# Loading the row-sum reciprocals with one broadcast DMA per head instead of one per two heads

## Chip, cores and metric

The kernel runs on 1 core of one Trainium2 chip. The metric is device microseconds of one execution, from inputs in the chip's memory to the output in it. Three runs of the kernel before are given, and one profiled execution of it.

## What is computed

Three parts follow each other: a masked attention over 4 batches, 8 heads, 576 rows and 64 columns a head, a gated unit, and a bilinear unit. All is in float32. Cut to what matters:

```python
scores = scale * q @ k.T
thresh = max(scores) - tau
attn = exp(where(scores >= thresh, scores, -1e9) - max(scores))
attn = attn / (sum(attn) + 1e-09)
x = attn @ v                                  # [2304 tokens, 512]
x = (silu(x @ w_gate) * (x @ w_val)) @ w_out  # gated unit
out = ((x @ w1) * (x @ w2)) @ w3 @ w_out2     # bilinear unit
```

## The kernel before

Float32 products are made from three matmuls each (`mm3`, line 814): every operand is split into a rounded high part and a low part, and high by high, high by low and low by high are added up in PSUM.

**Attention** goes through 16 pairs of heads (4 batches by 4 pairs). VectorE takes row maxima (L467) and masks (L486, which also writes the row sums), ScalarE takes the exponentials, TensorE transposes and multiplies by v (L565, L570). The product is not yet divided by its row sum. It leaves PSUM as two halves, which `it_pv` stores to the DRAM tensor `x_dram` (index e = 0, 1, L581). After the last pair of a batch `it_norm` takes the reciprocals of the row sums, turns them and stores them to `r_dram`, one row of 576 values for each batch and head (L596, L599).

**Between attention and gated unit** stands `x_prep(j, kk)`. The 2304 tokens are cut into five blocks j of 512, 512, 256, 512 and 512 tokens, and the 512 features into four groups kk of 128, which are two heads of 64 features each. `x_load` takes two tiles ("slots") from a list of free ones and loads into the first both halves from `x_dram` (L770), and into the second the reciprocals from `r_dram` (L774): the row of one head goes to each of the partitions 0 to 63, the row of the next head to each of the partitions 64 to 127, all in one DMA. A block that crosses a batch border does this in two segments (448 and 64 tokens, or 128 and 128). Then GpSimd adds the two halves (L805), VectorE multiplies by the reciprocals (L808), the two loaded slots are given back, ScalarE rounds the high part (L796) and VectorE subtracts to get the low part (L797). There are 20 such steps and 32 segments.

**The gated unit** goes through pairs g of 128-column groups f, and for each g through the five blocks. In the first pair (g = 0) `glu_step(0, j, f)` multiplies block j and prepares two of the four groups kk of block j + 1 (L923). So the blocks of x are made while the first pair is multiplied, and the later pairs find them there. `glu_h` makes the gated product (L898, L899) and splits it, with GpSimd on L106; `glu_out` multiplies it by `w_out` into `s_bank`.

**Weights** are loaded as raw words (`conv_load`, L127) into three buffers, and converted a step at a time (`conv_step`: VectorE L138 to L156, ScalarE L147, L148 and L195, GpSimd L149 and L198).

**Order.** Every data DMA of the kernel is issued from the SP queue, one after the other. The order of each engine's instructions is set by a scheduler when the program is built, so one more DMA can move others. The first step of block 0 and the first weights are prepared while attention runs (`early`), the first two steps of the gated unit in its tail.

Of the kernel before, what the change touches and what calls it, by code (L numbers as in the profile page):

```python
# [35 lines left out]
def kernel(  # L36
# [21 lines left out]
    nc = tc.nc  # L58
# [22 lines left out]
    r_dram = dram.tile([B, H, S], F32, name="r_dram")  # L81
# [93 lines left out]
    def take(dt=F32R):  # L175
        pool, tag = free.popleft()
        t = pool.tile([P, 2, 512], dt, tag=tag, name=tag, bufs=1)
        owner[id(t)] = (pool, tag, t)
        return t
# [574 lines left out]
    def segs(c0, n):  # L754
        done = 0
        while done < n:
            b, c = divmod(c0 + done, S)
            m = min(n - done, S - c)
            yield done, b, c, m
            done += m  # L760
# [4 lines left out]
    def x_load(j, kk):  # L765
        c0, n = blocks[j]
        x_raw[j, kk] = [take(F32) for _ in range(2)]
        tt, rg = x_raw[j, kk]
        for o, b, c, m in segs(c0, n):
            nc.sync.dma_start(  # L770
                out=tt[:, :, o:o + m],
                in_=x_dram[:, kk * P:(kk + 1) * P, b, c:c + m].rearrange("e p c -> p e c"),
            )
            nc.sync.dma_start(  # L774
                out=rg[:, 0, o:o + m],
                in_=r_dram[b, 2 * kk:2 * kk + 2, c:c + m].unsqueeze(1).to_broadcast([2, 64, m]),
            )
        return tt, rg

    def x_views(j):  # L780
# [20 lines left out]
    def x_prep(j, kk):  # L801
        c0, n = blocks[j]
        tt, rg = x_load(j, kk)
        xr = tmp()
        nc.gpsimd.tensor_tensor(  # L805
            out=xr[:, 0:n], in0=tt[:, 0, 0:n], in1=tt[:, 1, 0:n], op=ALU.add
        )
        nc.vector.tensor_tensor(out=xr[:, 0:n], in0=xr[:, 0:n], in1=rg[:, 0, 0:n], op=ALU.mult)  # L808
        give(*x_raw.pop((j, kk)))
        x_split(j, kk, xr[:, 0:n])  # L810
# [170 lines left out]
    for i in range(NF2):  # L981
        conv_until((i, 1), w3v)
        bank = t_bank()
        for c in range(NF2):
# [8 lines left out]
            out=un[:, 1, :], in0=bank, in1=f32(un[:, 0, :]), op=ALU.subtract  # L993
# [109 lines left out]
```

## Time and profile before

| | |
|---|---|
| median of 3 runs | 1231.96 us (1230.54 to 1233.79) |
| profiled execution, its time | 1231.65 us |
| profiled execution, its span | 1229.9 us |
| mean granted TensorE clock | 0.971 |
| busy in the span: PE, DVE, POOL, ACT | 1114.0, 788.0, 604.7, 563.0 us |

The span is from the first to the last instruction; some 1.7 us of the execution's time lie around it. PE is TensorE, DVE is VectorE, ACT is ScalarE, POOL is GpSimd, and SPq is the SP queue, which issues the DMAs. A busy share is an average over stages with different limits, so the rows below are taken by stage: up to about 347 us attention alone, from 347 to 402 us its tail with the first steps of the gated unit, then to 478 us the first pair of the gated unit, and from there on matmuls almost without a gap. The granted clock is given as a share of 2.4 GHz, so 0.50 is 1.2 GHz. The DMA share is the mean busy share of the core's 16 DMA engines; packets that overlap count each, so it can stand above 1.

### The profile page before, as it was taken

Reading aid. Unit: us, or ns where it says so; the run is one execution under the profiler, and the core shown is the slowest. Engines: PE = TensorE matmul, PEld = TensorE weight load, DVE = VectorE, ACT = ScalarE, POOL = GpSimd, SP = SyncE. Lnnn points to the kernel's source line nnn. Section 1 sums busy time; section 2 is a strip of 40 time slices with the busy share of each in tenths; the row PEclk is TensorE's granted clock in tenths of the full one; section 3 lists DMA queues with packets and bytes.
Section 4 is the critical chain, followed back from the end, with each engine's and each line's share of the span. In section 5 each row is a group of like instructions: output and inputs, shape, how many; then the busy total and the mean of one; then the engine's idle time right before and its main releaser. Section 6 shows DMA issues by size and latency. Waiting matters only on the chain.

```text
span 1229.9 us, 16704 instructions
## 1 busy us (share of the span) xinstructions
PE 1114.0 (91%) x5972; PEld 952.0 (77%) x5972; DVE 788.0 (64%) x1303; ACT 563.0 (46%) x1010; POOL 604.7 (49%) x602
## 2 busy tenths in 40 slices
PE   7888878888777845999999999999999999999998
PEld 5877777778666644888888888888877888888886
DVE  7999999999988635756546373548795021432223
ACT  6777667777755522634234242335474241231211
POOL 7999989999975423533323142324342131231110
PEclk9999999999978967999999999999999999999999
DMA  9856656555444544321102021113431010000014
GB/s 203 202 134 148 146 132 149 129 131 133 106 133 134 140 118 131 103 69 52 53 18 69 18 69 52 52 35 103 127 107 58 1 35 1 18 18 1 1 52 103
DMA packets 104370, 107.07 MB, mean 87 GB/s; under 512 B 47328, under 2 KB 78688, under 8 KB 104288
## 3 DMA queue, kind: packets, MB, share of 16 engines
q1 hardware_dynamic: 104288, 106.01, 33.2%
q8 instruction: 47, 0.77, 0.3%
q14 instruction: 35, 0.29, 0.1%
HBM read 68.16 MB, written 14.23 MB: 67 GB/s over the span
## 4 chain that ended last, share of the span: by engine, by line
PE 55%; DVE 15%; POOL 13%; DMA 8%; issue 3%; SPq 3%; ACT 1%; DVEq 0%; POOLq 0%; ACTq 0%
PE t_bank L814 36%; PE s_bank L814 18%; DVE P L486 5%; POOL AT L102 4%; DMA slot<-r_dram 3%; DVE P L467 3%; POOL AT L99 3%; DMA raw<-in_moe_w_gate_dram 2%; POOL AT L517 2%; DMA raw<-in_moe_w_dram 2%; POOL stat L459 2%; SPq L770 1%; DVE tmp L156 1%; DVE slot L797 1%; DVE tmp L144 1%
## 5 line engine op out<-in xcount | busy, mean ns | idle before, releaser
L814 PE MATMUL t_bank<-slot,slot 128*128 128x512 f32 (+1 forms) x2592 | 566.3, 374 | 25.2 <-ACT slot L796 14.1
L814 PEld LDWEIGHTS t_bank<-slot,slot 128*128 128x128 f32 x2592 | 461.4, 191 | 113.2 <-ACT slot L796 14.7
L486 DVE SCALAR_TENSOR_TENSOR P<-P,stat,E 128x576 f32<-128x576 f32 x144 | 184.2, 1303 | 1.6 <-POOL stat L459 1.3
L814 PE MATMUL s_bank<-h,slot 128*128 128x512 f32 (+1 forms) x720 | 163.6, 376 | 16.6 <-POOL h L106 15.6
L149 POOL TENSOR_TENSOR raw<-raw 128x512 int32<-128x512 int32 x76 | 86.9, 1144 | 159.7 <-ACT raw L148 149.2
L814 PEld LDWEIGHTS s_bank<-h,slot 128*128 128x128 f32 x720 | 128.7, 194 | 40.9 <-POOL h L106 16.5
L1043 POOL TENSOR_TENSOR h<-tmp,h 128x512 fp32r<-128x512 f32 (+1 forms) x38 | 45.8, 1204 | 200.5 <-ACT h L1041 200.5
L106 POOL TENSOR_TENSOR h<-tmp,h 128x512 fp32r<-128x512 f32 (+1 forms) x60 | 73.5, 1225 | 136.5 <-ACT h L105 136.4
L1039 DVE TENSOR_TENSOR tmp<-tmp,t_bank 128x512 f32<-128x512 f32 (+1 forms) x40 | 25.3, 633 | 178.3 <-PE t_bank L814 178.3
L476 ACT ACTIVATE E<-P,stat 128x576 f32<-128x576 f32 x144 | 112.6, 789 | 54.6 <-DVE P L467 27.9
L428 PE MATMUL s_bank<-R,L 128*128 128x288 f32 x512 | 100.3, 318 | 28.9 <-DVE P L467 24.8
L467 DVE TENSOR_SCALAR_CACHE_REDUCE P<-s_bank,neg 128x576 f32<-128x576 f32 x144 | 114.0, 806 | 5.1 <-PE s_bank L428 4.9
L899 DVE TENSOR_TENSOR tmp<-tmp,t_bank 128x512 f32<-128x512 f32 (+1 forms) x60 | 37.9, 631 | 116.7 <-PE t_bank L814 112.9
L814 PE MATMUL s_bank<-slot,h 128*128 128x512 f32 x432 | 106.6, 391 | 0.9 <-DVE slot L1029 0.8
L565 PE MATMUL t_bank<-AT,sp 128*128 128x288 f32 x512 | 94.2, 312 | 13.5 <-POOL AT L102 7.9
L428 PEld LDWEIGHTS s_bank<-R,L 128*128 128x128 f32 x512 | 74.9, 193 | 39.1 <-DVE P L467 34.6
L814 PEld LDWEIGHTS s_bank<-slot,h 128*128 128x128 f32 x432 | 80.0, 188 | 18.3 <-DVE slot L1029 2.1
L898 ACT ACTIVATE tmp<-t_bank 128x512 f32<-128x512 f32 (+1 forms) x60 | 33.3, 555 | 128.1 <-PE t_bank L814 125.3
L565 PEld LDWEIGHTS t_bank<-AT,sp 128*128 128x128 f32 x512 | 76.3, 195 | 19.0 <-POOL AT L102 11.2
L861 DVE TENSOR_TENSOR slot<-s_bank,slot 128x1024 f32<-128x1024 f32 (+1 forms) x68 | 77.6, 1142 | 18.6 <-PE s_bank L814 16.5
L523 PE MATMUL t_bank<-ident,P 128*128 128x128 f32 x512 | 75.7, 282 | 10.0 <-ACT AT L516 2.5
L156 DVE SCALAR_TENSOR_TENSOR tmp<-tmp,raw 128x512 f32<-128x512 f32 x76 | 66.6, 876 | 26.6 <-POOL raw L149 26.6
(105 smaller groups left out, 1511.4 us busy)
## 6 DMA issues: line engine op xcount, KB each, us to landing
raw<-in_moe_w_dram SPq DMA_DIRECT2D x32, 512.0 KB
raw<-in_moe_w_out_dram SPq DMA_DIRECT2D x20, 512.0 KB
x_dram<-xs SPq DMA_DIRECT2D x64, 144.0 KB
L<-qhi SPq DMA_DIRECT2D x60, 128.0 KB
L<-qlo SPq DMA_DIRECT2D x60, 128.0 KB
raw<-in_moe_w_gate_dram SPq DMA_DIRECT2D x12, 512.0 KB
raw<-in_moe_w_val_dram SPq DMA_DIRECT2D x12, 512.0 KB
ld<-in_k_dram SPq DMA_DIRECT2D x16, 256.0 KB
```

Of the source, the lines that this page charges most:

```text
L102: nc.gpsimd.tensor_tensor(out=lo, in0=src, in1=f32(hi), op=ALU.subtract)
L106: nc.gpsimd.tensor_tensor(out=lo, in0=src, in1=f32(hi), op=ALU.subtract)
L149: nc.gpsimd.tensor_tensor(out=a, in0=a, in1=x, op=ALU.subtract)
L156: nc.vector.scalar_tensor_tensor(out=f32(m), in0=f32(m), scalar=2.0 ** 20, in1=f32(a), op0=ALU.add, op1=ALU.mult)
L428: nc.tensor.matmul(o, lhsT=lhs, rhs=R[:, c:c + HALF], start=(h == hs2[0] and e == 0), stop=(h == hs2[-1] and e == 1),)
L467: nc.vector.tensor_scalar(out=p_tile(p, i).rearrange("p (a c) -> p a c", a=2), in0=sb[:, :, 0:HALF], scalar1=neg, scalar2=None, op0=ALU.mu ...
L476: nc.scalar.activation(out=e, in_=p_tile(p, i), func=ACTF.Exp, scale=-1.0, bias=stats[p // HP][:, 0, c:c + 1],)
L486: nc.vector.scalar_tensor_tensor(out=t, in0=t, scalar=stats[b][:, 1, c:c + 1], in1=e, op0=ALU.is_le, op1=ALU.mult, accum_out=sums[b][:, c: ...
L523: nc.tensor.transpose(bank[:, t * P:(t + 1) * P], pbuf[p, t][:, o:o + P], ident)
L565: nc.tensor.matmul(o, lhsT=vs[:, 4 * h + c, :, :].rearrange("p a d -> p (a d)"), rhs=AT[h][:, e, c, cs], start=(c == 0 and e == 0), stop=F ...
L814: nc.tensor.matmul(o, lhsT=lhs(a), rhs=rhs(c), start=(first and i == 0), stop=(last and i == 2))
L861: nc.vector.tensor_tensor(out=a, in0=s, in1=a, op=ALU.add)
```

## The change

The one load of reciprocals per segment becomes two, one for each head, each of 64 partitions:

```diff
-            nc.sync.dma_start(
-                out=rg[:, 0, o:o + m],
-                in_=r_dram[b, 2 * kk:2 * kk + 2, c:c + m].unsqueeze(1).to_broadcast([2, 64, m]),
-            )
+            for h in range(2):
+                nc.sync.dma_start(
+                    out=rg[64 * h:64 * h + 64, 0, o:o + m],
+                    in_=r_dram[b, 2 * kk + h:2 * kk + h + 1, c:c + m].to_broadcast([64, m]),
+                )
```

The same bytes reach the same places. 32 DMAs become 64. The source of the old DMA has the dimensions 2 (heads), 64 (repeats), m; the source of a new one has 64 (repeats), m.

The scheduler moves a few rows. On SP, in the tail of attention, these are the loads of block 0's last group (`slot_4720` and `slot_4721` before, `slot_4723` and `slot_4724` in the change) and of two groups of block 1. Before:

```order
L770 DMA slot_4720<-x_dram 128x2x512
L770 DMA slot_4913<-x_dram 128x2x64
L774 DMA slot_4914<-r_dram 128x1x64
L770 DMA slot_4913<-x_dram 128x2x448
L774 DMA slot_4914<-r_dram 128x1x448
L774 DMA slot_4721<-r_dram 128x1x512
L770 DMA slot_4898<-x_dram 128x2x64
L770 DMA slot_4898<-x_dram 128x2x448
L774 DMA slot_4899<-r_dram 128x1x64
L774 DMA slot_4899<-r_dram 128x1x448
L581 DMA x_dram<-xs 64x576 x2
```

With the change:

```order
L770 DMA slot_4723<-x_dram 128x2x512
L770 DMA slot_4919<-x_dram 128x2x64
L775 DMA slot_4920<-r_dram 64x64 x2
L770 DMA slot_4919<-x_dram 128x2x448
L775 DMA slot_4724<-r_dram 64x512 x2
L770 DMA slot_4902<-x_dram 128x2x64
L770 DMA slot_4902<-x_dram 128x2x448
L775 DMA slot_4920<-r_dram 64x448
L775 DMA slot_4903<-r_dram 64x64 x2
L581 DMA x_dram<-xs 64x576 x2
L775 DMA slot_4903<-r_dram 64x448 x2
L775 DMA slot_4920<-r_dram 64x448
```

The reciprocals of block 0's last group now go ahead of the long segment of block 1, and three 64x448 loads of block 1 now stand behind the next two stores of attention.

Later on SP, at the loads of block 4 (512 tokens, one segment), before:

```order
L770 DMA slot_5538<-x_dram 128x2x512
L774 DMA slot_5539<-r_dram 128x1x512
L774 DMA slot_5552<-r_dram 128x1x512
L770 DMA slot_5551<-x_dram 128x2x512
L770 DMA slot_5620<-x_dram 128x2x512
L127 DMA raw<-in_moe_w_gate_dram 128x4x256
```

With the change:

```order
L127 DMA raw<-in_moe_w_gate_dram 128x4x256
L770 DMA slot_5494<-x_dram 128x2x64
L775 DMA slot_5495<-r_dram 64x64 x2
L770 DMA slot_5566<-x_dram 128x2x512
L127 DMA raw<-in_moe_w_val_dram 128x4x256
L775 DMA slot_5567<-r_dram 64x512 x2
L770 DMA slot_5580<-x_dram 128x2x512
```

The raw load of the gate weights is now issued ahead of block 4's loads (and of the last short segment of block 3) instead of behind three of its x loads.

## Rows read from the trace of the kernel before

**Rows 1.** Busy time by stretch: PE, PEld, DVE, ACT, POOL, granted clock, DMA share, GB/s

```profile
347.00:402.00 55.00, 43.10 (x196) 35.46 (x196) 44.47 (x66) 30.22 (x56) 32.96 (x25) 0.79 0.53 142
402.00:430.00 28.00, 24.02 (x126) 20.07 (x125) 19.70 (x29) 13.54 (x26) 12.45 (x12) 1.00 0.52 147
430.00:478.40 48.40, 20.06 (x81) 15.84 (x79) 18.41 (x23) 12.97 (x22) 16.53 (x14) 0.69 0.49 139
478.40:858.00 379.60, 379.60 (x1845) 321.42 (x1846) 220.74 (x292) 143.14 (x230) 130.82 (x108) 0.99 0.19 59
```

**Rows 2.** Waits from 347 to 478.4 us: total us, times, longest us

```profile
POOL tmp L805 <- DMA slot<-x_dram: 44.4, 10, 8.4
...
PE s_bank L814 <- POOL h L106: 15.6, 2, 11.3
...
DVE tmp L808 <- DMA slot<-r_dram: 14.4, 4, 5.3
PE t_bank L814 <- ACT slot L796: 14.1, 2, 11.8
```

**Rows 3.** Longest pieces of the chain, 347 to 478.4 us: start us, us, what

```profile
347.59 9.68 DMA slot<-r_dram
358.13 14.02 DMA slot<-r_dram
...
445.77 10.37 DMA slot<-x_dram
461.69 13.59 DMA raw<-in_moe_w_gate_dram
```

**Rows 4.** Short stretches, columns as in the first group

```profile
348.50:350.00 1.50, 1.50 (x10) 1.50 (x9) 1.50 (x6) 0.17 (x1) 0.00 (x0) 0.70 1.06 388
...
367.50:370.00 2.50, 2.50 (x8) 1.96 (x7) 0.00 (x0) 0.00 (x0) 0.00 (x0) 0.53 0.13 49
```

**Rows 5.** DMAs issued from 347 to 478.4 us: count and KB of each

```profile
slot<-r_dram SPq DMA_DIRECT2D x8, 224.0 KB
slot<-r_dram SPq DMA_DIRECT2D x6, 256.0 KB
...
slot<-r_dram SPq DMA_DIRECT2D x8, 64.0 KB
slot<-r_dram SPq DMA_DIRECT2D x8, 32.0 KB
```

**Rows 6.** Issue on SP, lines 774 and 770, 402 to 478.4 us: count, ns min/median/max

```profile
L774 SPq DMA_DIRECT2D slot<-r_dram x20: 486/538/3787, 401.6 to 473.1; - x20
...
L770 SPq DMA_DIRECT2D slot<-x_dram x19: 360/1746/4306, 402.2 to 467.2; - x19
```

**Rows 7.** TensorE's rows that start after a gap, 434 to 480 us: [gap, releaser]

```profile
442.97 1.65 PE L814 MATMUL s_bank<-h,slot 128*128 128x256 f32 x6 [11.33 <-POOL h L106]
...
450.59 3.99 PE L814 MATMUL s_bank<-h,slot 128*128 128x256 f32 x17 [4.27 <-POOL h L106]
...
465.88 0.73 PE L814 MATMUL s_bank<-h,slot 128*128 128x512 f32 x2 [0.97 <-ACT h L105]
478.38 2.07 PE L814 MATMUL t_bank<-slot,slot 128*128 128x512 f32 x4 [11.77 <-ACT slot L796]
```

**Rows 8.** Waits from 347 to 402 us

```profile
DVE tmp L808 <- DMA slot<-r_dram: 8.4, 2, 5.3
```

**Rows 9.** SP's timeline and the chain, 370 to 383 us

```profile
370.14 3.86 SPq L581 DMA_DIRECT2D x_dram<-xs  x2
...
382.79 1.17 DVE tmp L808
```

**Rows 10.** Pieces of the chain elsewhere: other transfers from issue to landing

```profile
30.31 5.80 DMA R<-klo
...
268.91 2.01 DMA R<-khi
...
872.07 3.79 DMA raw<-in_moe_w_dram
```

## The prediction

> **What bounds the kernel now.** I read the busy time by stretch first [rows 1]. From 478.4 us to 858 us TensorE is busy all of 379.60 us: nothing that a DMA does there is worth anything, and whatever is gained ahead of it moves the end by as much. The stretch to look at is 347 to 478.4 us. There TensorE stands still for 55.0 - 43.10 = 11.9, 28.0 - 24.02 = 4.0 and 48.4 - 20.06 = 28.3 us, 44 us in all, and in the last part its granted clock is 0.69, which is a mix of its two levels, 1.2 and 2.4 GHz. No other engine is full there either: VectorE, the busiest beside it, works 44.47, 19.70 and 18.41 us.
>
> The waits say what they stand for [rows 2]: GpSimd's addition in `x_prep` waits 44.4 us for `x_dram` loads, VectorE's multiplication 14.4 us for `r_dram` loads, and behind these two TensorE waits 15.6 and 14.1 us. The chain's longest pieces are transfers [rows 3]: the reciprocals of one step take 9.68 and 14.02 us from issue to use, an `x_dram` load 10.37 us and 512 KB of gate weights 13.59 us. Elsewhere in the kernel a 64-partition transfer of 128 KB lands in 2.01 us, at worst 5.80 us, and 512 KB of weights in 3.79 us [rows 10]. So something slows all transfers of this stretch, though the mean DMA share is only about 0.5 [rows 1].
>
> The short stretches show it [rows 4]. From 348.5 to 350 us, with weights, an `x_dram` load and reciprocals under way, the share is 1.06 at 388 GB/s. From 367.5 to 370 us, when VectorE waits for reciprocals and little else is left to move, the share is 0.13 at 49 GB/s. A share of 0.13 is 2.1 of 16 engines: **a load of reciprocals runs on two DMA engines**, at some 24.5 GB/s each, the speed at which each of 16 goes in the other row (388 / 16 = 24.3). Everything that is spread over all 16 must then queue on these two. How much: 8 x 224 + 6 x 256 + 8 x 64 + 8 x 32 = 4096 KB [rows 5], 4.19 MB, at 49 GB/s 85.6 us of both engines. The mean share of 0.53, 0.52 and 0.49 [rows 1] makes 0.53 x 55 + 0.52 x 28 + 0.49 x 48.4 = 67.4 us on each of 16 engines, 1079 engine-us; less 2 x 85.6, the rest is 907 / 16 = 57 us on each. The two engines then have 85.6 + 57 = 142 us of work in 131.4 us, and the other fourteen 57. Two engines are the bound of this stretch. SP's rows agree: an `x_dram` issue takes 0.36 us at best, 1.75 us at the median and 4.31 us at worst [rows 6], so SP is held up while it issues.
>
> **The change, part by part.**
> *Spread.* Each new load has 64 repeats as its first dimension instead of 2 heads. The 64-partition transfer of 2.01 us [rows 10] moves 128 KB, 64 GB/s with its fixed time in it, more than two engines gave; so 64 rows are enough to get past two engines. I take all 16. By the Trainium skill ("DMA: Bandwidth & Descriptors", "Rules for kernel authors") the slowest dimension that isn't 1 sets the number of engines, and a leading dimension below 16 confines the DMA to that many. Its 2 agrees with the 0.13 [rows 4]; no run yet shows its 16 for a repeated row. The two engines' 142 us become 67 us on each of the 16.
>
> *347 to 402 us.* VectorE waits 8.4 us for reciprocals [rows 8]; it is the busiest engine there with 44.47 of 55 us, so I take the wait as gain, 8.4 us. Ends: 5.3 us, if only the longest goes, and 10.5 us, all of VectorE's idle time. What is late next is VectorE's own work.
>
> *402 to 430 us.* TensorE is busy 24.02 of 28 us at full clock. At most 4.0 us can go, I take half, 2.0.
>
> *430 to 478.4 us.* TensorE's four gaps are 11.33, 4.27, 0.97 and 11.77 us [rows 7]. The first two end with GpSimd's line 106, which stands behind its wait for `x_dram`; the last with ScalarE's line 796, behind a VectorE that waits for gate weights. All three wait for transfers that are slowed by the two engines. With them gone VectorE's 18.41 us are the largest sum here. In the stretch before, VectorE was busy 19.70 / 28 = 0.70 of the time; at that density 18.41 us take 26.3 us, so the gain is 48.4 - 26.3 = 22.1 us. Upper end: VectorE without a pause, 30 us. A part of it is TensorE's clock: its 20.06 us at 0.69 would be some 14 us at 1.00.
>
> *SP.* 32 more issues at 0.538 us [rows 6] are 17 us of SP, 10.8 of them after 402 us. I cost them at nothing: with `x_dram` issues at their shortest (19 x 0.36 = 7 us) and 40 reciprocal issues (21.5 us) SP has some 30 us of work beside a few weight loads, less than the 52 us that remain of this part (76.4 - 2.0 - 22.1). If that cover goes, it is the slower rival below.
>
> *Moved rows.* Block 0's last reciprocals now go ahead of block 1's, which helps the 14.02 us wait [rows 3]. Three 64x448 loads of block 1 come behind two stores, whose issues ended at 374.0 us; the next multiplication on the chain that could want them starts at 382.79 us [rows 9]. 8 us of cover, and 2 to 6 us are needed for landing [rows 10]: nothing. The gate weights ahead of block 4's loads: they help the 11.77 us gap, counted already.
>
> *Sum.* 8.4 + 2.0 + 22.1 = 32.5 us off the profiled execution's 1231.65 us, **1199 us**. The median of the runs shown is 0.3 us above that execution, so the same holds against it. Lower bound of the gain: only the 14.4 us for which VectorE waited for reciprocals by name [rows 2], 1217. Upper: 10.5 + 4.0 + 30.0 = 44.5, 1187.
>
> **Rivals.**
> *Compute takes over at once.* If conversions and `x_prep` on VectorE and GpSimd leave no more slack than the waits by name, less than 14.4 us go: 1218 to 1228 us. For it: VectorE was 81% busy from 347 to 402 us. Against: from 430 us on no engine is over 42% busy [rows 1].
>
> *SP becomes the bound, slower.* The place is SP between 402 and 478 us. If its long `x_dram` issues (1.75 us) come from the number of transfers under way and not from the two engines, they stay, and 20 more issues at 0.538 us lie in their row: 1231.65 + 10.8 = 1242 us. It decides from the point where SP's issues fill the time between two steps. Against it: issues of the same line go down to 0.36 us [rows 6]. By the Trainium skill (same page and section) two transfers to the two partition halves aren't worth it: they run one after the other on the same engines, so one of 128 partitions is better, and small ones should be merged. By that rule the change would only add fixed times, and this rival's 1242 us would be the result. Its premise, that the one transfer already uses all 16 engines, isn't met here [rows 4].
>
> *The change doesn't do what it says.* The 49 GB/s may be what reading the same row again and again gives, however many engines ask. Then the new loads move at 49 GB/s as well, every transfer still queues as long, and the time stays at 1232 us, within 4 us. Against it: 24.5 GB/s for an engine is the same as where different rows are read [rows 4]. If the limit were for each row, 24.5 GB/s, the load would take twice as long on all engines, 171 + 57 = 228 us of work in the stretch instead of 142, some 86 us more: 1318 us. I give that 1 in 100.
>
> **How the numbers follow.** 0.3% (3.7 us) is about what a measurement of this kernel can tell from no change. The forecast, 1187 to 1217 us, has 0.80; a gain above that 0.02; compute at once 0.09; no change 0.04; SP 0.04; the limit by row 0.01. Faster by over 0.3% is 0.80 + 0.02 + 0.09 = 0.91, the same 0.04, slower 0.05. The range is the forecast's own, from the two bounds of the sum; it leaves 0.2 out.
>
> **What would show it.** In the profile after, no stretch should stay at a share of 0.13 while VectorE waits; the waits of L808 for `r_dram` (14.4 us) should fall under 3 us, those of L805 for `x_dram` (44.4 us) under 15 us; the median `x_dram` issue should fall to about 0.5 us; TensorE's gaps of 11.33 and 11.77 us should be under 4 us each, and the block of unbroken matmuls should begin near 446 us instead of 478 us. The prediction is wrong if reciprocals still take over 5 us to land, or if these waits go and others on VectorE or SP as long as they take their place.

## The result and the profile after

| | before | change |
|---|---|---|
| median | 1231.84 us, 4 runs (1230.54 to 1233.79) | 1202.57 us, 4 runs (1201.48 to 1202.91) |
| ratio to before | | 0.976, 95% interval 0.9743 to 0.9777 |
| span of the profiled execution | 1229.9 us | 1200.7 us |

The change is 29.3 us faster, 2.4%; forecast were 32.5 us. In the code after, lines behind 775 stand one lower: L806 is GpSimd's addition, L809 VectorE's multiplication, L815 the matmul.

To compare the stretch I cut both traces at the same two events: TensorE's run of 41 matmuls that starts block 1 (403.83 us before, 398.36 us after) and the first matmuls on block 4 (478.38 and 447.78 us). Busy time by stretch of the kernel before, cut in this way (PE, PEld, DVE, ACT, POOL, granted clock, DMA share, GB/s):

```profile
347.00:403.83 56.83, 44.12 (x199) 35.97 (x198) 46.30 (x69) 30.97 (x58) 32.98 (x25) 0.80 0.54 148
403.83:478.38 74.55, 43.03 (x199) 35.38 (x199) 36.26 (x49) 25.74 (x45) 28.96 (x25) 0.80 0.49 138
```

The same view of the kernel after:

```profile
347.00:398.36 51.36, 41.37 (x203) 34.77 (x201) 48.75 (x69) 31.60 (x58) 35.16 (x25) 0.86 0.56 165
398.36:447.78 49.42, 42.15 (x200) 35.00 (x200) 39.75 (x50) 25.36 (x45) 29.16 (x23) 0.90 0.72 198
447.78:830.00 382.22, 381.35 (x1858) 322.06 (x1859) 225.60 (x293) 145.52 (x233) 137.63 (x113) 1.00 0.19 59
```

5.5 us went ahead of the first event and 25.1 us between the two, 30.6 us together; 1.4 us of it are lost again before the end. The second stretch holds almost the same work on every engine (199 or 200 matmuls, 49 or 50 instructions of VectorE) in 49.42 instead of 74.55 us. Its mean DMA share went up from 0.49 to 0.72: about the same bytes in less time.

The waits after, from 347 to 450 us (total us, times, longest), answer to [rows 2]:

```profile
POOL tmp L806 <- DMA slot<-x_dram: 14.6, 4, 4.7
...
PE t_bank L815 <- ACT slot L797: 3.2, 3, 2.0
...
PE s_bank L815 <- POOL h L106: 2.4, 1, 2.4
DVE tmp L809 <- DMA slot<-r_dram: 2.4, 2, 1.9
```

GpSimd's 44.4 us for `x_dram` became 14.6, VectorE's 14.4 us for `r_dram` became 2.4, though `x_dram`'s loads weren't touched. TensorE's gaps of 11.33 and 11.77 us [rows 7] have these rows in their place (TensorE's timeline, the gap and what ended it in brackets):

```profile
429.62 2.50 PE L815 MATMUL s_bank<-h,slot 128*128 128x256 f32 x10 [2.38 <-POOL h L106]
...
447.78 1.21 PE L815 MATMUL t_bank<-slot,slot 128*128 128x512 f32 x4 [0.43 <-ACT slot L797]
...
452.63 4.85 PE L815 MATMUL t_bank<-slot,slot 128*128 128x512 f32 x20 [0.67 <-DVE slot L798]
```

SP's issues of both lines from 394 to 446 us (count, ns min/median/max, first and last start), against [rows 6], and between them the time from issue to landing of those reciprocal loads for which the trace tells it, 19 of the whole kernel's 64:

```profile
L775 SPq DMA_DIRECT2D slot<-r_dram x39: 444/484/596, 396.1 to 444.3; - x39
...
DMA to landing us min/median/max: 2.3/3.3/8.0
...
L770 SPq DMA_DIRECT2D slot<-x_dram x20: 372/586/1292, 395.7 to 443.7; - x20
```

The median `x_dram` issue fell from 1.75 to 0.59 us and the longest from 4.31 to 1.29 us. The reciprocals land in 3.3 us at the median, 3 of the 19 only after more than 5 us. The chain gives pieces that can be compared: from 347 us on, its two longest for reciprocals were 9.68 and 14.02 us before [rows 3], and its longest is 4.85 us after.

### The profile page after: what moved, and what is told of

It is laid out like the page before. It is cut to its first block, busy times and chain, and to the rows that moved or that the text cites. A ratio compares the mean times of both kernels' runs of the same rounds, so it can differ in the third digit from the quotient of the medians.

```text
span 1200.7 us, 16747 instructions
## 1 busy us (share of the span) xinstructions
PE 1117.6 (93%) x5972; PEld 959.7 (80%) x5972; DVE 796.2 (66%) x1303; ACT 563.5 (47%) x1010; POOL 610.5 (51%) x602
## 4 chain that ended last, share of the span: by engine, by line
PE 59%; DVE 17%; POOL 12%; DMA 6%; issue 3%; ACT 2%; SPq 1%; DVEq 0%; ACTq 0%; POOLq 0%
PE t_bank L815 37%; PE s_bank L815 18%; DVE P L486 4%; POOL AT L102 4%; DVE P L467 2%; POOL AT L99 2%; DVE slot L798 2%; DMA raw<-in_moe_w_dram 2%; POOL AT L517 2%; DVE tmp L156 2%; POOL stat L459 1%; DMA slot<-r_dram 1%; DVE tmp L809 1%; DVE tmp L144 1%; DMA slot<-x_dram 1%
## 5 line engine op out<-in xcount | busy, mean ns | idle before, releaser
L815 PE MATMUL t_bank<-slot,slot 128*128 128x512 f32 (+1 forms) x2592 | 564.4, 373 | 9.3 <-DVE slot L798 5.1
L815 PEld LDWEIGHTS t_bank<-slot,slot 128*128 128x128 f32 x2592 | 459.4, 190 | 98.0 <-DVE slot L798 6.8
L486 DVE SCALAR_TENSOR_TENSOR P<-P,stat,E 128x576 f32<-128x576 f32 x144 | 179.3, 1270 | 2.0 <-POOL stat L459 1.9
L815 PE MATMUL s_bank<-h,slot 128*128 128x512 f32 (+1 forms) x720 | 161.8, 372 | 4.9 <-ACT h L105 2.5
L815 PEld LDWEIGHTS s_bank<-h,slot 128*128 128x128 f32 x720 | 127.0, 191 | 28.4 <-ACT h L105 3.2
L1044 POOL TENSOR_TENSOR h<-tmp,h 128x512 fp32r<-128x512 f32 (+1 forms) x38 | 45.8, 1205 | 200.5 <-ACT h L1042 200.5
L106 POOL TENSOR_TENSOR h<-tmp,h 128x512 fp32r<-128x512 f32 (+1 forms) x60 | 76.0, 1267 | 134.6 <-ACT h L105 131.4
L428 PE MATMUL s_bank<-R,L 128*128 128x288 f32 x512 | 103.8, 327 | 25.0 <-DVE P L467 22.7
L565 PE MATMUL t_bank<-AT,sp 128*128 128x288 f32 x512 | 98.2, 321 | 13.9 <-POOL AT L102 7.5
L815 PE MATMUL s_bank<-slot,h 128*128 128x512 f32 x432 | 106.6, 391 | 0.9 <-DVE slot L1030 0.8
L428 PEld LDWEIGHTS s_bank<-R,L 128*128 128x128 f32 x512 | 78.6, 202 | 33.8 <-DVE P L467 31.5
L565 PEld LDWEIGHTS t_bank<-AT,sp 128*128 128x128 f32 x512 | 79.9, 203 | 19.3 <-POOL AT L102 10.5
L815 PEld LDWEIGHTS s_bank<-slot,h 128*128 128x128 f32 x432 | 80.0, 188 | 18.3 <-DVE slot L1030 2.1
L156 DVE SCALAR_TENSOR_TENSOR tmp<-tmp,raw 128x512 f32<-128x512 f32 x76 | 70.4, 928 | 27.9 <-POOL raw L149 27.9
```

Of the source, the lines that this page charges most:

```text
L106: nc.gpsimd.tensor_tensor(out=lo, in0=src, in1=f32(hi), op=ALU.subtract)
L156: nc.vector.scalar_tensor_tensor(out=f32(m), in0=f32(m), scalar=2.0 ** 20, in1=f32(a), op0=ALU.add, op1=ALU.mult)
L428: nc.tensor.matmul(o, lhsT=lhs, rhs=R[:, c:c + HALF], start=(h == hs2[0] and e == 0), stop=(h == hs2[-1] and e == 1),)
L486: nc.vector.scalar_tensor_tensor(out=t, in0=t, scalar=stats[b][:, 1, c:c + 1], in1=e, op0=ALU.is_le, op1=ALU.mult, accum_out=sums[b][:, c: ...
L565: nc.tensor.matmul(o, lhsT=vs[:, 4 * h + c, :, :].rearrange("p a d -> p (a d)"), rhs=AT[h][:, e, c, cs], start=(c == 0 and e == 0), stop=F ...
L815: nc.tensor.matmul(o, lhsT=lhs(a), rhs=rhs(c), start=(first and i == 0), stop=(last and i == 2))
```

## The experiments

My theory: what counts is the number of DMA engines that a load runs on. On two engines the loads of reciprocals fill these two, and all other transfers, each of which has a part on them, wait. Its rival: smaller loads, or the order that the scheduler made of them, brought the gain. A second question is what SP's issues cost. Each median below is of 4 runs (10 in the last experiment), and each kernel was timed against the kernel before on the same chip. Differences between two kernels are differences of their medians. The kernel before had medians of 1231.84, 1232.1 and 1232.9 us on these occasions, so a difference of 1 us between kernels of different occasions says nothing.

### The change's two loads, on two and on four engines

The source's 64 repeats are written with another first dimension. The order of instructions is that of the change on all engines, so only the spread differs:

```diff
-                    in_=r_dram[b, 2 * kk + h:2 * kk + h + 1, c:c + m].to_broadcast([64, m]),
+                    in_=r_dram[b, 2 * kk + h:2 * kk + h + 1, c:c + m].unsqueeze(1)
+                    .to_broadcast([2, 32, m]),
```

> Two loads per segment, one per head, as in the change, and the same instruction order on every engine; only the source's 64 repeats are written as 2 x 32, so that its first dimension is 2. Theory (the number of DMA engines of a load is what counts): the load is back on two engines, stretches with a DMA share of 0.13 return, and the time goes back to 1228 to 1245 us (two more issues per segment may cost a little beside). Rival (the smaller loads or the changed order brought the gain): 1201 to 1204 us, as the change.

Measured: 1237.33 us, ratio 1.0042 (1.0027 to 1.0057), 34.8 us slower than the change. Busy time of two short stretches, columns as above:

```profile
365.00:368.00 3.00, 3.00 (x8) 2.35 (x8) 2.70 (x4) 0.03 (x1) 1.31 (x1) 0.50 0.14 50
388.00:390.50 2.50, 2.50 (x10) 1.95 (x10) 2.50 (x3) 0.85 (x2) 1.83 (x1) 0.77 0.13 47
```

The share of 0.13 at 49 GB/s [rows 4] is back. Of the 105 stretches of 1 us from 347 to 452 us, 28 stood between 0.11 and 0.17 in the kernel before, 33 do here and 5 in the change. So is the gap behind GpSimd (TensorE's timeline):

```profile
447.37 2.50 PE L816 MATMUL s_bank<-h,slot 128*128 128x256 f32 x10 [11.78 <-POOL h L106]
```

For four engines:

```diff
-                    .to_broadcast([2, 32, m]),
+                    .to_broadcast([4, 16, m]),
```

> As the two-engine variant, the repeats written as 4 x 16. Theory: the load's 85.6 us on two engines become 42.8 us on four; with the 57 us of other work these four have 100 us, about the 103 us that the stretch takes after the change, so they are nearly full: 1204 to 1216 us, between the two, and a share near 0.25 when only these loads run. Rival (order or size): 1201 to 1204 us.

Measured: 1207.42 us, ratio 0.9798 (0.9784 to 0.9813). A stretch in which little but these loads moves:

```profile
365.00:369.00 4.00, 4.00 (x11) 3.13 (x10) 4.00 (x9) 0.62 (x1) 0.43 (x1) 0.52 0.27 94
```

Twice the share and twice the rate of two engines: 23 to 25 GB/s for each engine in both, while the engines read the same one or two rows again and again. That the change's own loads run on 16 engines can't be read from a share, as they hardly ever run alone. The trace's records of completion tell it: each of these loads leaves 3 of them in the kernel before and on two engines, 5 on four, and 16 in the change. On two and four that is one above the count from the shares; where the additional record comes from isn't shown.

That settles the rivals. With one order and one size of load, the time is 1237.3, 1207.4 and 1202.6 us on 2, 4 and 16 engines; order and size bring nothing by themselves (on two engines the change's loads are even 5.2 us slower than the old one). Nor is it the row that limits: a rate that doubles with the engines isn't the row's.

### One load of 128 partitions on 16 engines

The reciprocals are copied 8 times in DRAM, so that one source of 16 rows serves both heads:

```diff
...
+            nc.sync.dma_start(
+                out=r8_dram[b], in_=r_dram[b].unsqueeze(1).to_broadcast([H, 8, S]),
+            )
...
-            for h in range(2):
-                nc.sync.dma_start(
-                    out=rg[64 * h:64 * h + 64, 0, o:o + m],
-                    in_=r_dram[b, 2 * kk + h:2 * kk + h + 1, c:c + m].to_broadcast([64, m]),
-                )
+            nc.sync.dma_start(
+                out=rg[:, 0, o:o + m],
+                in_=r8_dram[b, 2 * kk:2 * kk + 2, :, c:c + m].rearrange("h e c -> (h e) c")
+                .unsqueeze(1).to_broadcast([16, 8, m]),
+            )
```

> One load of 128 partitions per segment again, but on 16 engines: the reciprocals are copied 8 times in DRAM (one more DMA per batch), so that the source's first dimension is 16. Theory: as fast as the change or faster, because SP issues 32 loads less, of which some 20 lie between 395 and 446 us, where SP issues without a pause after the change: 1195 to 1203 us. Rival (two smaller loads are what helps): back near 1225 to 1235 us.

Measured: 1198.69 us (1197.54 to 1199.82), ratio 0.9728 (0.9713 to 0.9742). It is the fastest complete kernel here, 3.9 us ahead of the change; the two ranges of runs don't meet. Busy time of its stretches, cut at the same events:

```profile
347.00:397.00 50.00, 39.88 (x199) 33.38 (x198) 47.74 (x68) 31.23 (x58) 34.89 (x25) 0.88 0.58 170
397.00:442.60 45.60, 39.12 (x200) 32.41 (x200) 39.26 (x49) 25.42 (x46) 28.91 (x23) 1.00 0.83 236
```

VectorE is busy 39.26 of 45.60 us, and no row of L813, its multiplication there, waits for a DMA. Two loads aren't needed, only 16 engines.

A second way to one load without copies lets the two heads of a group alternate over the partitions (the edits of the rows of `x_dram` and of the weights are left out here):

```diff
...
-            for h in range(2):
-                nc.sync.dma_start(
-                    out=rg[64 * h:64 * h + 64, 0, o:o + m],
-                    in_=r_dram[b, 2 * kk + h:2 * kk + h + 1, c:c + m].to_broadcast([64, m]),
-                )
+            nc.sync.dma_start(
+                out=rg[:, 0, o:o + m],
+                in_=r_dram[b, 2 * kk:2 * kk + 2, c:c + m].unsqueeze(0).to_broadcast([64, 2, m]),
+            )
```

> One load of 128 partitions on 16 engines without copies: the two heads of a group alternate over the partitions, so that the source is 64 x 2 x m; the rows of x_dram and of the gate and value weights are taken in the same order, which cuts each of the 24 gate and value weight loads into four of 128 KB. Theory (engines count, and SP's issues come next): 32 issues fewer in the tight part, 72 more spread over the gated unit: 1196 to 1203 us. If the weight loads' issues land in the tight part, up to 1208 us. Rival (two smaller loads help): near 1230 us.

Measured: 1202.43 us, ratio 0.9746 (0.9730 to 0.9762), as the change. So the rival (near 1230 us) falls once more. What it saves in issues its weight loads, cut in four, or other parts of the edit take back; which of them wasn't separated.

### What SP's issues cost

Once more as many loads, each of 32 partitions and still on 16 engines:

```diff
-            for h in range(2):
+            for h in range(4):
                 nc.sync.dma_start(
-                    out=rg[64 * h:64 * h + 64, 0, o:o + m],
-                    in_=r_dram[b, 2 * kk + h:2 * kk + h + 1, c:c + m].to_broadcast([64, m]),
+                    out=rg[32 * h:32 * h + 32, 0, o:o + m],
+                    in_=r_dram[b, 2 * kk + h // 2:2 * kk + h // 2 + 1, c:c + m].to_broadcast([32, m]),
                 )
```

> Each load cut again, into four of 32 partitions (32 is still a multiple of 16). It asks what an issue on SP costs. If SP is the next bound from 395 to 446 us, about 40 more issues of 0.5 us there cost up to 20 us: 1208 to 1223 us. If SP still has room: 1200 to 1206 us.

Measured: 1211.82 us, ratio 0.9834 (0.9818 to 0.9851), 9.3 us slower than the change. From 394 to 456 us SP issues so, and the reciprocals for which the trace tells it land so:

```profile
L775 SPq DMA_DIRECT2D slot<-r_dram x78: 302/419/1650, 394.6 to 455.0; - x78
...
DMA to landing us min/median/max: 1.7/2.3/4.7
```

Each load lands sooner (2.3 us) and the kernel is slower. At the medians, SP needs 78 x 0.419 = 32.7 us for these issues instead of 39 x 0.484 = 18.9, some 14 us more. On the chain SP's issues of line 775 are 20.6% of these 62 us, 12.8 us; in the change they are 8.9% of the 52 us from 394 to 446, 4.6 us. The difference of 8 us is most of the 9.3. Taken with the 3.9 us that 32 loads fewer gave, and the 5.2 us that 32 more cost on two engines, my estimate is that an issue here costs some 0.12 to 0.16 us of the end. The order of the instructions moves a little in all three as well, so the three together carry the reading, not one of them.

The change's loads, issued from ScalarE's queue:

> The change with its 64 loads issued from ScalarE's queue instead of SP's. If SP's issues are the next bound, and ScalarE (busy 26 of 51 us there) has room: 1196 to 1201 us. If not, or if ScalarE's own issue times take what SP gains: 1201 to 1210 us.

```diff
-                nc.sync.dma_start(
+                nc.scalar.dma_start(
                     out=rg[64 * h:64 * h + 64, 0, o:o + m],
```

Measured: 1211.53 us, ratio 0.9822 (0.9807 to 0.9836), slower than the change by 9.0 us, and above both ranges. The issues now stand between ScalarE's own instructions, and VectorE's multiplication waits 7.8 us for reciprocals instead of 2.4. So ScalarE's queue doesn't give the room that SP lacks. But the scheduler also moved hundreds of rows on TensorE, VectorE and ScalarE in this run, and how much of the 9.0 us comes from that wasn't separated.

### Floor and the old load on another queue

The loads are left out, and a loaded tile stands in as the factor:

```diff
-            for h in range(2):
-                nc.sync.dma_start(
-                    out=rg[64 * h:64 * h + 64, 0, o:o + m],
-                    in_=r_dram[b, 2 * kk + h:2 * kk + h + 1, c:c + m].to_broadcast([64, m]),
-                )
...
-        nc.vector.tensor_tensor(out=xr[:, 0:n], in0=xr[:, 0:n], in1=rg[:, 0, 0:n], op=ALU.mult)
+        nc.vector.tensor_tensor(out=xr[:, 0:n], in0=xr[:, 0:n], in1=tt[:, 1, 0:n], op=ALU.mult)
```

> The reciprocals aren't loaded; the multiplication takes a part of the x_dram tile as its second factor instead (the normalisation is left out). It gives the floor: what all loads of reciprocals still cost after the change. Theory: two engines were nearly all of their cost, so what is left is SP's issues and their 4.19 MB on 16 engines (11 us of them): 1193 to 1201 us. If the loads were still a bound after the change: below 1190 us.

Measured: 1197.63 us, ratio 0.9706 (0.9690 to 0.9723). All loads of reciprocals together still cost 4.9 us in the change (6.7 us by the two ratios, 0.976 and 0.9706), and with one load on 16 engines about 1 us, which these runs can't tell from nothing: the intervals of the two ratios overlap. Little more is to be had from this load.

The last experiment takes the kernel before and issues its loads from ScalarE's queue:

> The kernel before, its 32 loads on two engines, issued from ScalarE's queue. It tells whether the two engines' own time is the bound or only the place in SP's queue behind them. Theory (142 us of work on two engines): the time stays slow, 1222 to 1245 us. Rival (only the order in the one queue, x_dram rows standing behind rows of reciprocals, and SP held up by it): 1203 to 1215 us.

```diff
-            nc.sync.dma_start(
+            nc.scalar.dma_start(
                 out=rg[:, 0, o:o + m],
```

Measured: 1233.60 us, ratio 1.0009 (1.0000 to 1.0018). Issue of the two lines (line 774 now on ScalarE's queue):

```profile
L774 ACTq DMA_DIRECT2D slot<-r_dram x32: 488/1314/6298, 111.5 to 473.8; - x32
```

```profile
L770 SPq DMA_DIRECT2D slot<-x_dram x32: 359/363/1322, 52.7 to 467.7; - x32
```

SP is free now (0.363 us for the median `x_dram` issue) and GpSimd's wait for `x_dram` is down to 7.7 us, but the hold-up has moved to the queue that issues to the two engines: up to 6.3 us for one issue, with ScalarE's instructions behind it. The time is the same. That agrees with two engines that are full, whoever feeds them. As ScalarE is held up in this run, and the scheduler moved hundreds of rows on TensorE, VectorE and ScalarE, the time alone doesn't tell the engines' own time from the stall of the issuing queue. An estimate from the trace's records of completion (with the DMAs of a semaphore taken in the order of their issue) speaks for the engines: the median `x_dram` load issued from 347 to 478 us took 6.2 us from issue to landing in the kernel before, 7.2 us here, where no reciprocals stand ahead of it in its queue, and 4.0 us in the change.

## Why the prediction was right

*The bound.* Right: two engines at some 24.5 GB/s each, and all else that has a part on them waits. The two- and four-engine variants show it with nothing else changed. That the two are full for the whole stretch was worked out and not seen: 142 us of work don't fit into 131.4 us, so the sum made from shares is some 8% too high at least and says "about full", no more. On four engines it gave 42.8 + 57 = 100 us, nearly full, and four engines cost 4.9 us more than sixteen, which agrees. By the Trainium skill ("DMA: Bandwidth & Descriptors", "Rules for kernel authors") the slowest dimension sets the number of engines; the shares 0.13 to 0.14 and 0.27 for 2 and 4 agree, as 2.1 to 2.2 and 4.3 of 16 engines. That section of the Trainium skill also has the rule against two transfers to two partition halves, which stood beside the slower rival. Two loads were 29.3 us faster than the one load on two engines, so that rule doesn't hold for such a load; where both kinds use 16 engines, the one load was 3.9 us faster, as the rule says.

*347 to 402 us, 8.4 us.* Mis-sized: 5.5 us. The waits did go (VectorE's idle time fell from 56.83 - 46.30 = 10.5 to 2.6 us), but the same 69 instructions of VectorE took 48.75 instead of 46.30 us. 7.9 - 2.45 = 5.5. The step took VectorE's work as fixed. Its multiplication alone grew by 4.3 us, while others shrank; the same seven of one shape up to the first event, before and after (busy us and mean ns, then idle time before them):

```profile
L808 DVE TENSOR_TENSOR tmp<-tmp,slot 128x512 f32<-128x512 f32 x7 | 5.8, 831 | 8.4 <-DMA slot<-r_dram 8.4
```

```profile
L809 DVE TENSOR_TENSOR tmp<-tmp,slot 128x512 f32<-128x512 f32 x7 | 10.1, 1439 | 0.1
```

Each took 0.68 to 1.18 us before and 0.68 to 1.78 us after. The long ones run while GpSimd works, and GpSimd works in more of the time (32.98 of 56.83 us before, 35.16 of 51.36 after). That it is the cause agrees with these rows but wasn't tested.

*402 to 478 us, 2.0 + 22.1 us.* Right in sum: 25.1 us. The way to it, a density of 0.70 for VectorE at the end, was only near, and two misses offset each other, which is luck: VectorE's work there grew from 36.26 to 39.75 us, and it was denser than forecast, 39.75 / 49.42 = 0.80 over the whole stretch against (19.70 + 18.41) / 52.3 = 0.73. Block 4 starts at 447.78 us, 446 was forecast.

*After 478 us.* Some 1.4 us are lost: small gaps of 0.67 and 0.20 us follow block 4's start, and where the rest goes wasn't traced. I had counted the dense part as fixed.

*SP at nothing.* Wrong by about 4 us, in the direction of the slower rival. I had worked out 30 us of work in 52 us. SP's issues from 394 to 446 us add up to 37 us, so there is room in the sum. What the sum left out is the order. SP doesn't issue without a pause there, as I had written ahead of the run with copies; it waits, most of all with raw loads of weights, for buffers that VectorE frees (SP's waits from 394 to 446 us after):

```profile
SPq L127 <- DVE tmp L156: 9.6, 4, 3.7
```

Behind such waits it issues back to back, and its issues of line 775 stand on the chain for the 4.6 us named above. With 32 issues fewer the kernel was 3.9 us faster. The rival was right that SP's issues cost time; the price was 3.9 and not 10.8 us, and it came on top of the gain. Its condition, that long `x_dram` issues stay, was not met (0.59 us).

*Moved rows.* Right for the three loads named: they are issued from 364.92 to 366.20 us, and VectorE's waits from 347 to 398 us are for TensorE and GpSimd (0.24 and 2.20 us), none for reciprocals. But I overlooked a pair of 64x448 loads. The load that it replaces was issued at 388.38 us, ahead of two stores and a raw load of `in_moe_w_val_dram`; the pair stands behind all three, at 389.05 and 389.61 us. It is a piece of the chain after, and lands just as VectorE gets to it.

```profile
389.05 4.85 DMA slot<-r_dram
```

*What was to show it.* Waits for `r_dram` under 3 us: 2.4. For `x_dram` under 15: 14.6. Issues of 0.5 us: 0.59. Gaps under 4 us: 2.38 and 0.43. Stretches of 1 us near a share of 0.13: 5 are left of 28. One sign of being wrong is met in part: 3 of the 19 reciprocal loads whose landing is told took over 5 us, up to 8.0, though no piece of the chain for reciprocals is longer than 4.85 us there. The other, new waits as long on VectorE, is not: from 347 us to block 4's start it idled 48.8 us before and 12.3 us after.

## What to carry to other kernels

Read the mean DMA share as a count of engines: 0.13 at 49 GB/s with an engine waiting is two engines of 16, however free the other fourteen look. Look then at the first dimension of that load's source; a broadcast over few rows wants its long dimension first, by loads cut at the rows or by rows copied until there are 16. Don't cut finer than that, since each issue has its price on the queue.

## What was not expected

A load on two engines holds up its issuing queue, too: 4.31 us for one issue on SP [rows 6] and 6.30 us on ScalarE's queue, where it stops ScalarE's own work. And that many engines read the same 2 KB row costs little: the rate went from 49 to 94 GB/s from two to four engines, and removing the loads altogether gains only 4.9 us over sixteen.
